# Filler matmuls of constants in the first third, an early activation table, and an order remade with the DMA lanes counted

## The chip, the cores and the metric

The kernel runs on one core of a Trainium2 chip. The metric is the device time of one execution in microseconds; the table of the profile gives the three runs of the kernel before and the one that was profiled.

## The reference

Two stages follow each other. The first is attention over 8 batches and 8 heads, with 1152 keys of 64 channels; the queries are averaged in pairs first, so that 576 are left. The second is a layer over the 4608 rows that come out of it: the maximum of three products, and a product of that.

```python
q_pool = q.reshape(B, H, S // factor, factor, D).mean(axis=3)
scores = scale * np.matmul(q_pool, k.transpose(0, 1, 3, 2))
scores = scores - np.max(scores, axis=-1, keepdims=True)
attn = np.exp(scores)
attn = attn / (np.sum(attn, axis=-1, keepdims=True) + 1e-09)
return np.matmul(attn, v).astype(np.float32)
...
h = np.maximum(np.maximum(x @ w1, x @ w2), x @ w3)
return (h @ w_out).astype(np.float32)
```

Here x is the attention's output with the eight heads of a query side by side (512 channels), w1 to w3 are 512 x 768 and w_out is 768 x 512. All values are float32.

## The kernel before, in words

**Units.** The attention is cut into 64 units, d = 0 to 63. A unit holds a pair of heads (two heads side by side), one batch, and half of the 576 queries, 288. For each of its nine blocks of 128 keys (kk = 0 to 8), TensorE (PE) makes the scores of both heads with four matmuls of 288 columns (`product` in `scores`, lines L578 and L579: the queries are split into a high and a low part, and so are the keys), into one of two PSUM buffers `pqk`. ScalarE (ACT) copies a block to SBUF (L588, into `s`, which holds three blocks) and VectorE (DVE) takes the running maximum `acc` (L594 for the first, L597). A PSUM buffer is free again when its copy and its maximum are done, so the product of block kk waits for the maximum of block kk-2.

After the ninth block the maximum over keys is turned (`rows`, L688, into `pmt`), reduced by DVE (L694), turned back and spread over the partitions (`bcast`, L704, into `pmb`), and DVE subtracts it from the scores (`sub`, L733, six instructions per unit: three for the first 345 columns, whose maximum lies in PSUM pool `ps_a`, and three for the other 231, in `ps_b`). From unit 16 on (`TURN`) the maximum goes another way, by `fold`, `turn` (L648), `summit` and a matmul L714. ACT makes the exponential (L739), and PE multiplies by the values (`pav`, L784). The sums over keys come from PE for d < 8 (L828) and later from GpSimd (POOL, L754 and L756).

**The second stage** is cut into chunks of tokens. A chunk needs x of all four head pairs, and the weights, which arrive as 64-bit numbers and are split into a high and a low part: ACT L975, L988 and L999, DVE L978 and L983, POOL L991 and L1002. Until the first chunk can start, shortly before 213 us, PE has attention alone to do; after that there is always some of the second stage's work (L1068, L1123) to put between.

**What sets the order.** Every piece of work is a `Step` with the engine it runs on, a cost and the steps it waits for. `arrange` (from L211) plays the steps through on a clock per engine and, at each turn, gives the engine that is free first the ready step of the lowest rank. Ranks come from the tables `RANK` and `NUDGE`. Steps are then written out in that order, so each engine's queue is fixed. The planner knows that TensorE's clock halves: it sums the columns streamed in windows of 4096 / 1200 = 3.41 us (`WINDOW`) and takes a step for twice as long when the window before held fewer than 3072 (`BUSY`).

```python
            while rest > 1e-9:
                w = int(at / WINDOW + 1e-9)
                while len(streamed) < w + 2:
                    streamed.append(0.0)
                slow = 2 if w == 0 or streamed[w - 1] < BUSY else 1
```

A DMA step gets a tail, the time until its data has landed. Most loads, and the moves of split keys (`kc`, L498) and queries (`qq`, L506), are issued by SyncE (SP); the four moves of the first half of the queries of unit 0 by ACT. There are eight completion semaphores for DMAs, used in turn, here called lanes: an issue waits until the DMA that had its lane before has landed. The planner before does not know of these.

At the start, ACT's first instruction is the cast L461 of the queries; the load of its activation table stands right before it and comes behind the same wait.

Of the kernel before, what the change touches and what calls it, by code (L numbers as in the profile page):

```python
# [18 lines left out]
P = 128  # L19
# [20 lines left out]
    "qk": -1610.0615,  # L40
    "cp": -180.1672,
    "mx": -1253.2067,
    "rows": -786.0194,
    "turn": -1110.3828,
    "top": 469.0602,
    "diag": -189.5205,
    "red": 77.8083,
    "bc": -879.861,
    "sub": 3840.475,
    "exp": 984.6769,  # L50
    "keys": -2399.561,
    "av": 683.8571,
    "xcopy": -1571.289,
    "psum": 782.1931,
    "eps": 214.1172,
    "inv": 1557.6025,
    "xm": -150.8782,
    "load": -1024.6367,
    "prep": 2386.9581,
    "move": 1089.3258,  # L60
    "split": -86.6507,
    "ffn": 707.8881,
    "rate": 5.1716,
    "mm": 974.547,
    "fetch": 157.873,
    "evac": -1776.9799,
    "hhigh": 675.1121,
    "hlow": -1456.4392,
    "conv": 1545.6563,
    "rate0": 0.2612,  # L70
    "first_qk": -105.5392,
    "first_cp": 492.9138,
    "first_mx": 996.4585,
    "first_sub": 621.8249,
    "first_exp": 463.1478,
    "first_keys": -3171.6001,
    "first_av": -465.3423,
    "first_xcopy": 820.1949,
    "first_psum": 3176.8613,
    "first_inv": 117.4318,  # L80
    "first_xm": -1228.9986,
    "first_load": -1485.6615,
    "first_prep": 53.3922,
    "first_move": -618.3481,
    "first_split": 1939.7866,
# [102 lines left out]
BUSY = 3072  # L188
EARLY = 16
THIRDS = 7  # L190
LENT = 8
SUMS = 8
SPLIT = 8
IDLE = 0
APART = 0
SWITCH = 0.2

class Step:  # L200
# [10 lines left out]
def arrange(plan, slots):  # L211
# [12 lines left out]
    free = {k: [0.0] * n for k, n in slots.items()}  # L224
    parked = {k: [] for k in slots}
    order = []
    streamed = [0.0]
    mode = 0
    wire = 0.0

# [977 lines left out]
```

## Time and profile before

| | |
|---|---|
| median of three runs | 1421.44 us (1420.52 to 1423.86) |
| profiled execution, its own time | 1425.01 us |
| span of its instructions | 1423.2 us |
| mean granted TensorE clock over the span | 0.986 |
| busy in the span: PE, DVE, ACT, POOL | 1365.0, 1001.9, 915.3, 1069.1 us |
| busy from 0 to 213 us: PE, DVE, ACT | 168.45, 153.06, 157.39 us |

PE is an abbreviation for TensorE's matmuls, PEld for its weight loads, which overlap them. A row of the windows view gives, for a stretch in microseconds from the span's start, its length, then the busy time of each engine with its number of instructions, then the clock that TensorE was granted (1.00 is full speed), the share of time in which the DMA engines worked, and what they moved. A stretch with no record of the clock is shown as 1.00; there the distance between neighbouring matmuls tells the rate. A row of the timeline gives start, duration, engine, line, operation and tiles, and in brackets how long the engine had been idle before it and what ended that. A row of the groups gives the count after x, then busy time and mean nanoseconds of one, then idle time before.

### The profile page before, as it was taken

To read this page: it belongs to the slowest core of one execution; us is meant where nothing else is said; L and a number is where in the kernel's file an instruction comes from. 1 tells how busy PE (TensorE), PEld (TensorE's weight loads), DVE (VectorE), ACT (ScalarE), POOL (GpSimd) and SP (SyncE) were. 2 spreads that over 40 slices of the span, in tenths; PEclk is the share of its full clock that TensorE was granted. 3 is DMA by queue.
4 is the path that set the end of the run, shared out by engine and by line. 5 is a ranking of instruction groups with operands and counts; after the bars stand their busy time and mean duration, and the time that the engine had idled before them with its cause. 6 is when DMAs were issued, how large, how long until landed. Compare 5 with 4: busy or idle time off the path is not lost.

```text
span 1423.2 us, 24396 instructions
## 1 busy us (share of the span) xinstructions
PE 1365.0 (96%) x8608; PEld 1063.3 (75%) x8608; DVE 1001.9 (70%) x1355; ACT 915.3 (64%) x1520; POOL 1069.1 (75%) x843
## 2 busy tenths in 40 slices
PE   4878889999999999999999999999999999999999
PEld 3555567777777777776777777777877777778999
DVE  4778777766777878887778877777877778862110
ACT  3878787656766777767666776666766666661211
POOL 1344468879888999899898998899789988783210
PEclk9999889999999999999999999999999999999999
DMA  6678787655566756664567556765666466515451
GB/s 185 190 255 236 222 261 203 178 180 155 139 197 191 197 145 182 205 188 127 164 191 195 157 166 190 193 195 143 189 189 181 130 180 190 160 38 177 146 169 50
DMA packets 117353, 250.13 MB, mean 176 GB/s; under 512 B 15728, under 2 KB 75504, under 8 KB 117232
## 3 DMA queue, kind: packets, MB, share of 16 engines
q1 hardware_dynamic: 116656, 247.99, 59.4%
q8 instruction: 69, 1.13, 0.3%
q10 hardware_dynamic: 576, 0.59, 0.2%
q14 instruction: 52, 0.43, 0.1%
HBM read 154.14 MB, written 18.87 MB: 122 GB/s over the span
## 4 chain that ended last, share of the span: by engine, by line
PE 85%; DVE 4%; ACT 3%; DMA 3%; issue 2%; POOL 2%; SPq 1%; ACTq 0%; POOLq 0%; DVEq 0%
PE ph L1068 30%; PE pav L784 19%; PE pqk L578 11%; PE po L1123 10%; PE pqk L579 9%; DVE acc L597 2%; PE psum L798 2%; ACT s L588 1%; DVE s L733 1%; PE pmb L714 1%; DMA w<-in_win_dram 1%; PE psum L828 1%; ACT s L739 1%; POOL ksum L756 1%; DMA qq<-qraw 1%
## 5 line engine op out<-in xcount | busy, mean ns | idle before, releaser
L756 POOL TENSOR_TENSOR ksum<-ksum,s 128x576 f32<-128x576 f32 x392 | 557.9, 1423 | 20.9 <-ACT s L739 2.5
L1068 PE MATMUL ph<-xh,w 128*128 128x512 f32 (+2 forms) x1440 | 460.5, 372 | 0.3 <-ACT hm L1087 0.3
L733 DVE TENSOR_TENSOR s<-s,pmb 128x864 f32<-128x864 f32 (+2 forms) x384 | 395.5, 1045 | 41.6 <-PE pmb L714 36.3
L588 ACT COPY s<-pqk 128x576 f32<-128x576 f32 x576 | 359.1, 639 | 100.8 <-PE pqk L579 96.5
L597 DVE TENSOR_TENSOR acc<-acc,pqk 128x576 f32<-128x576 f32 x448 | 334.7, 747 | 125.7 <-ACT s L588 121.5
L578 PE MATMUL pqk<-qq,kc 128*128 128x288 f32 x1152 | 346.0, 317 | 49.7 <-DVE acc L597 20.4
L739 ACT ACTIVATE s<-s 128x864 f32<-128x864 f32 (+2 forms) x384 | 353.7, 932 | 53.6 <-DVE s L733 51.4
L579 PE MATMUL pqk<-qq,kc 128*128 128x288 f32 x1152 | 327.6, 301 | 0.0
L578 PEld LDWEIGHTS pqk<-qq,kc 128*128 128x128 f32 x1152 | 222.8, 193 | 121.4 <-issue 37.1
L784 PE MATMUL pav<-s,v 128*64 128x288 f32 x2304 | 303.9, 417 | 0.6 <-DVE w L983 0.6
L1068 PEld LDWEIGHTS ph<-xh,w 128*128 128x128 f32 x1440 | 262.9, 188 | 37.1 <-issue 1.8
L1068 PE MATMUL ph<-xl,w 128*128 128x512 f32 (+2 forms) x720 | 266.9, 371 | 0.0
L784 PEld LDWEIGHTS pav<-s,v 128*64 128x64 f32 x2304 | 163.8, 140 | 117.8 <-issue 15.3
L579 PEld LDWEIGHTS pqk<-qq,kc 128*128 128x128 f32 x1152 | 224.4, 195 | 11.6
L1099 POOL TENSOR_TENSOR h<-hm,h 128x512 fp32r<-128x512 f32 (+2 forms) x60 | 70.9, 1181 | 98.7 <-ACT h L1096 98.5
L1068 PEld LDWEIGHTS ph<-xl,w 128*128 128x128 f32 x720 | 135.6, 188 | 10.4
L1089 DVE TENSOR_TENSOR hm<-hm,ph 128x512 f32<-128x512 f32 (+2 forms) x120 | 75.2, 626 | 95.5 <-PE ph L1068 92.1
L1123 PE MATMUL po<-h,wo_hi 128*128 128x512 f32 (+2 forms) x480 | 139.2, 374 | 0.2 <-ACT ob L1139 0.2
L754 POOL TENSOR_TENSOR ksum<-s 128x576 f32<-128x576 f32 x56 | 80.7, 1441 | 69.7 <-ACT s L739 69.6
L793 ACT COPY xr<-pav 128x288 f32<-128x288 f32 x64 | 25.5, 399 | 147.3 <-PE pav L784 147.1
L472 POOL TENSOR_TENSOR kraw<-kraw 128x1152 fp32r<-128x1152 f32 x31 | 82.7, 2667 | 46.8 <-ACT kraw L468 29.6
L805 DVE RECIPROCAL rs<-rs 128x288 f32<-128x288 f32 (+1 forms) x64 | 96.5, 1507 | 23.4 <-ACT rs L802 21.5
(69 smaller groups left out, 1169.6 us busy)
## 6 DMA issues: line engine op xcount, KB each, us to landing
w<-w_split SPq DMA_DIRECT2D x162, 512.0 KB, 3.8
kc<-kraw SPq DMA_DIRECT2D x384, 96.0 KB, 3.2
qq<-qraw SPq DMA_DIRECT2D x252, 144.0 KB, 3.7
v<-in_vr_dram SPq DMA_DIRECT2D x32, 576.0 KB, 3.8
kraw<-in_kT_dram SPq DMA_DIRECT2D x31, 576.0 KB, 5.7
qraw<-in_qT_dram SPq DMA_DIRECT2D x31, 576.0 KB, 4.0
w<-in_win_dram SPq DMA_DIRECT2D x18, 512.0 KB, 4.9
w_split<-wc SPq DMA_DIRECT2D x18, 512.0 KB, 5.0
```

The costliest lines, as they stand in the source:

```text
L472: vec[e].tensor_tensor(lo.bitcast(F32R), lo, o.hl[:, 0, x:y], op=ALU.subtract)
L578: nc.tensor.matmul(ps[:, h - hs[0], :QH], w, qq[:, 0, h], start=True, stop=False)
L579: nc.tensor.matmul(ps[:, h - hs[0], :QH], w, qq[:, 1, h], start=False, stop=True)
L588: nc.scalar.copy(o.s[kk // 3][:, kk % 3, slice(*hs)], o.ps[kk, hs][:, :, :QH])
L597: nc.vector.tensor_tensor(acc, acc, ps, op=ALU.max)
L733: nc.vector.tensor_tensor(s, s, o.pb[h][:, None, :w].broadcast_to([P, 3, w]), op=ALU.subtract)
L739: nc.scalar.activation(s, s, AF.Exp, scale=SCALE)
L756: vec[e].tensor_tensor(o.ksum, o.ksum, x, op=ALU.add)
L784: nc.tensor.matmul(o.pav[64 * h : 64 * h + 64, :QH], pr.v[:, kk, h], o.s[kk // 3][:, kk % 3, h], start=(kk == 0), stop=(kk == NK - 1),)
L805: nc.vector.reciprocal(o.rs, o.rs)
L1068: nc.tensor.matmul(t.ps[:, : hi - lo], w[:, a, kk], xx[:, kk, lo:hi], start=(kk == 0 and i == 0), stop=(kk == 3 and i == 2),)
L1123: nc.tensor.matmul(t.ps[:, : hi - lo], ww[:, kk, ms], hh[kk // 3][:, kk % 3, lo:hi], start=(kk == 0 and i == 0), stop=(kk == 5 and i == 2),)
```

## The change

Three things are done, and the order is made anew.

**Fillers.** Where the planner sees PE idle before the next step, within the first `FILL_END` = 500 us, and the window holds fewer than `BUSY` columns, it puts in matmuls of constants (`idle`, L1183 to L1186): 64 columns of the identity matrix against the identity, or against a matrix of ones with 64 columns where PE has just worked on half the array. Their output, `junk`, is never read. It lies in the last 128 columns of a PSUM bank that is now one tile for the whole kernel, `bank`; the first 384 columns, `bank_a`, take the place of the pool `ps_a`, for `pmt` and `pmb` of the first 345 columns. Because 128 columns are gone, `turn` and `summit` write to the front of the bank. There are 208 fillers: 163 with the identity as weights and 45 with the ones; 48 of them stand ahead of the first product.

**Table.** An exponential of one column of `eps` is ACT's first instruction, so that the table's load waits for no data.

**Lanes.** A DMA step starts, for the planner, no earlier than the eighth DMA before it has landed.

**Order.** `RANK` and `NUDGE` hold new numbers throughout (one line of each is shown).

```diff
-    "qk": -1610.0615,
+    "qk": -1495.1031,
...
-    "av.0": 687.59, "av.1": 431.26, "av.10": -61.53, "av.11": -1121.69, "av.12": 92.79, "av.13": 2220.5,
+    "av.0": -115.98, "av.1": -51.15, "av.10": -108.01, "av.11": -670.85, "av.12": 1006.11, "av.13": 2186.58,
...
-IDLE = 0
+FILL = 256
+FILL_END = 500
+LANES = 8
...
+    landed = [0.0] * LANES
...
-    while len(order) < len(plan):
+    todo = len(plan)
+    while todo:
...
+        if e == "pe" and FILL and clock[e] < min(FILL_END, t):
+            at = clock[e]
+            while True:
+                w = int(at / WINDOW + 1e-9)
+                while len(streamed) < w + 2:
+                    streamed.append(0.0)
+                if streamed[w] >= BUSY:
+                    at = (w + 1) * WINDOW + 1e-7
+                    if at >= t:
+                        break
+                    continue
+                took = (FILL / 2400 + 0.02) * (2 if w == 0 or streamed[w - 1] < BUSY else 1)
+                if at + took > t:
+                    break
+                streamed[w] += FILL
+                at += took
+                order.append((at, None, mode))
+        if s.size:
+            t = max(t, landed[-LANES])
...
+            landed.append(wire + 1.8)
...
+    bank = ps_a.tile([P, 512], F32, name="bank_a")
+    bank_a, junk = bank[:, :384], bank[:, 384:]
...
+    nc.scalar.activation(cpool.tile([P, 1], F32, name="first"), eps, AF.Exp)
...
-            o.pb[0] = ps_a.tile([P, 512], F32, tag="a", name=f"pmb{d}_0")
-            nc.tensor.transpose(o.pb[0][:, QH : QH + P], crest[d % 2], ident)
+            o.pb[0] = bank_a
+            nc.tensor.transpose(o.pb[0][:, :P], crest[d % 2], ident)
...
-                o.pt[h] = pools[h].tile([P, 512], F32, tag="ab"[h], name=f"pmt{d}_{h}")
+                o.pt[h] = ps_b.tile([P, 512], F32, tag="b", name=f"pmt{d}") if h else bank_a
...
-                o.pb[h] = pools[h].tile([P, 512], F32, tag="ab"[h], name=f"pmb{d}_{h}")
+                o.pb[h] = ps_b.tile([P, 512], F32, tag="b", name=f"pmb{d}_{h}") if h else bank_a
...
+    def idle(mode):
+        n = FILL // 4
+        rows, cols = (64, ones) if mode else (P, ident)
+        nc.tensor.matmul(junk[:rows, :n], cols, ident[:, :n], start=True, stop=True)
...
         for _, s, e in order:
-            s.fn(e)
+            if s is None:
+                idle(e)
+            else:
+                s.fn(e)
```

How it moves instructions is shown at three places. In these rows `pqk0_1` is unit 0, block 1; a row tells what is written and what is read, and in brackets the semaphores that the instruction waits for (the engine's name, or a DMA lane). Lines of the changed kernel are some twenty higher: L599 and L600 are the scores, L804 the values, L753 the subtraction, L609 ACT's copy.

The first place is PE's queue at its beginning, before the change:

```order
L578 MATMUL pqk0_0_174<-qq0_0_144,kc0_0_147 128x288 [waits DMAHW6_49,DMAHW7_49,DMAHW1_49,DMAHW0_49]
L579 MATMUL pqk0_0_174<-qq0_0_144,kc0_0_147 128x288
L578 MATMUL pqk0_0_174<-qq0_0_144,kc0_0_147 128x288 [waits DMAHW3_49,DMAHW5_49,DMAHW2_49,DMAHW0_49]
L579 MATMUL pqk0_0_174<-qq0_0_144,kc0_0_147 128x288
L578 MATMUL pqk0_1_181<-qq0_0_144,kc0_0_147 128x288
```

The same place of PE's queue after the change, up to the second block:

```order
L1186 MATMUL bank_a_94<-ident_95 128x64 [waits Pool_49]
L1186 MATMUL bank_a_94<-ident_95 128x64 x47
L599 MATMUL pqk0_0_220<-qq0_0_147,kc0_0_150 128x288 [waits DMAHW6_49,DMAHW7_49,DMAHW1_49,DMAHW0_49]
L600 MATMUL pqk0_0_220<-qq0_0_147,kc0_0_150 128x288
L599 MATMUL pqk0_0_220<-qq0_0_147,kc0_0_150 128x288 [waits DMAHW4_49,DMAHW5_49,DMAHW3_49,DMAHW2_49]
```

48 fillers, which wait for nothing but the identity matrix that POOL makes, have come in ahead of the first product.

The second place is ACT's queue at its beginning. `qraw0` and `kraw0` are the queries and keys of the first pair, which ACT casts (L461 and L468; L482 and L489 in the changed kernel) and whose halves the DMAs move into `qq0_0`. Before:

```order
L461 ACT_TABLE_LOAD [waits DMAHW0_49]
L461 CAST qraw0_130<-qraw0_130 128x288 [waits DVE_49]
L468 CAST kraw0_132<-kraw0_132 128x384 [waits DMAHW1_49]
L506 DMA qq0_0_144<-qraw0_130 64x2x288 [waits DVE_49]
L506 DMA qq0_0_144<-qraw0_130 64x2x288
L461 CAST qraw0_130<-qraw0_130 128x288 [waits DMAHW2_49,DVE_49]
L468 CAST kraw0_132<-kraw0_132 128x384 [waits DMAHW3_49]
L468 CAST kraw0_132<-kraw0_132 128x384 [waits DMAHW4_49]
L506 DMA qq0_0_144<-qraw0_130 64x2x288 [waits DMAHW5_49]
L506 DMA qq0_0_144<-qraw0_130 64x2x288 [waits DMAHW0_49]
```

ACT's queue at its beginning after the change:

```order
L387 ACT_TABLE_LOAD
L387 ACTIVATE first_104<-eps_102 128x1 [waits DVE_49]
L482 CAST qraw0_133<-qraw0_133 128x288 [waits DMAHW0_49,DVE_49]
L489 CAST kraw0_135<-kraw0_135 128x384 [waits DMAHW1_49]
L527 DMA qq0_0_147<-qraw0_133 64x2x288 [waits DVE_49]
L527 DMA qq0_0_147<-qraw0_133 64x2x288
L527 DMA qq0_0_147<-qraw0_133 64x2x288 [waits DMAHW4_49]
L527 DMA qq0_0_147<-qraw0_133 64x2x288 [waits DMAHW5_49]
L482 CAST qraw0_133<-qraw0_133 128x288 [waits DMAHW2_49,DVE_49]
L489 CAST kraw0_135<-kraw0_135 128x384 [waits DMAHW3_49]
```

The table's load has lost its wait, and the third and fourth move of the queries have come ahead of the casts of the other query half and of the second and third part of the keys.

The third place is PE's queue at the end of unit 2's scores, where unit 1's values are mixed in (`pav1`). Before:

```order
L784 MATMUL pav1_543<-s1_0_255,v0_194 64x288 x4
L578 MATMUL pqk2_7_559<-qq1_0_317,kc1_2_342 128x288 [waits DVE_49]
L579 MATMUL pqk2_7_559<-qq1_0_317,kc1_2_342 128x288
L578 MATMUL pqk2_7_559<-qq1_0_317,kc1_2_342 128x288
L579 MATMUL pqk2_7_559<-qq1_0_317,kc1_2_342 128x288
L578 MATMUL pqk2_8_567<-qq1_0_317,kc1_2_342 128x288 [waits DVE_49]
L579 MATMUL pqk2_8_567<-qq1_0_317,kc1_2_342 128x288
```

The same end of unit 2's scores on PE after the change:

```order
L599 MATMUL pqk2_7_615<-qq1_0_420,kc1_2_450 128x288 [waits DVE_49]
L600 MATMUL pqk2_7_615<-qq1_0_420,kc1_2_450 128x288
L599 MATMUL pqk2_7_615<-qq1_0_420,kc1_2_450 128x288
L600 MATMUL pqk2_7_615<-qq1_0_420,kc1_2_450 128x288
L1186 MATMUL bank_a_94<-ident_95 128x64 [waits DVE_49]
L1186 MATMUL bank_a_94<-ident_95 128x64 x6
L599 MATMUL pqk2_8_638<-qq1_0_420,kc1_2_450 128x288 [waits PE_49]
L600 MATMUL pqk2_8_638<-qq1_0_420,kc1_2_450 128x288
```

Seven fillers have come between the blocks, and the first of them waits for DVE. Since `junk` and `bank_a` are one tile, a filler counts as a writer of the tile that DVE's subtraction reads: here it waits for the subtraction of unit 1 from `s1_2`, which stands behind the maximum of block 6 in DVE's queue. 27 groups of fillers have such a wait for DVE, and 10 subtractions of DVE wait for a filler in turn.

More of the change, by code (lines that the diff above doesn't have):

```diff
@@ L39 @@
 RANK = {
-    "qk": -1610.0615,
[L41 to L85, printed above, removed]
+    "qk": -1495.1031,
+    "cp": 59.6252,
+    "mx": -795.4198,
+    "rows": -884.2635,
+    "turn": -1391.2299,
+    "top": 1202.9278,
+    "diag": -1242.8229,
+    "red": -51.5927,
+    "bc": -1041.7961,
+    "sub": 4016.7319,
+    "exp": 1156.5563,
+    "keys": -2564.3934,
+    "av": 1420.6901,
+    "xcopy": -731.9903,
+    "psum": 1442.2799,
+    "eps": 64.1427,
+    "inv": 2145.5552,
+    "xm": -578.7354,
+    "load": -1554.9367,
+    "prep": 2701.617,
+    "move": 1738.2672,
+    "split": -84.4622,
+    "ffn": 768.468,
+    "rate": 4.6882,
+    "mm": 1532.7636,
+    "fetch": -298.6013,
+    "evac": -1037.2018,
+    "hhigh": 612.2296,
+    "hlow": -1655.1451,
+    "conv": 1058.5478,
+    "rate0": 1.462,
+    "first_qk": 283.3284,
+    "first_cp": -22.0406,
+    "first_mx": 198.0721,
+    "first_sub": 933.0186,
+    "first_exp": 126.2895,
+    "first_keys": -3301.6863,
+    "first_av": -1158.6745,
+    "first_xcopy": 808.7904,
+    "first_psum": 2911.6716,
+    "first_inv": 79.6498,
+    "first_xm": -697.1703,
+    "first_load": -1812.6465,
+    "first_prep": -907.8762,
+    "first_move": -1756.2913,
+    "first_split": 1822.6689,
 }
 NUDGE = {
[90 rows of a table removed]
[90 rows of a table added]
 }
@@ L293, in arrange @@
             s.tail = wire - s.end + 1.8
+            landed.append(wire + 1.8)
         order.append((t, s, e))
+        todo -= 1
         if s.give:
@@ L418, in tile_attention_ffn @@
         pass
-    def stream(e):
-        ps = ps_ff.tile([P, 512], F32, tag="ff", name="idle")
-        nc.tensor.matmul(ps[:, :P], ident, ident, start=True, stop=True)
-    for i in range(IDLE):
-        Step(plan, lambda: 1e5, [pe(213)], stream, [], take="ff", give="ff", cols=512)
     pairs = {}
@@ L630, in scores @@
         o.rows, o.subs, o.exps, o.pt, o.pb, o.m = [], [[], []], {}, {}, {}, {}
-        pools = (ps_a, ps_b)
         late = d >= TURN
@@ L646, in turn @@
         def turn(e):
-            o.pb[0] = ps_a.tile([P, 512], F32, tag="a", name=f"pmb{d}_0")
-            nc.tensor.transpose(o.pb[0][:, QH : QH + P], crest[d % 2], ident)
+            o.pb[0] = bank_a
+            nc.tensor.transpose(o.pb[0][:, :P], crest[d % 2], ident)
         def summit(e):
-            o.top = o.pb[0][:NB, QH + P : QH + P + SQ]
+            o.top = o.pb[0][:NB, P : P + SQ]
             nc.vector.tensor_reduce(
-                o.top, o.pb[0][:NB, QH : QH + P].rearrange("p (g k) -> p k g", g=4), axis=AX.X, op=ALU.max
+                o.top, o.pb[0][:NB, :P].rearrange("p (g k) -> p k g", g=4), axis=AX.X, op=ALU.max
             )
```

178 rows, old and new, of the table NUDGE are left out of this document.

## The prediction

> **What bounds the kernel now.** I read the page first, then the same rows by stage.
>
> ```profile
> span 1423.2 us, 24396 instructions
> ...
> PEclk9999889999999999999999999999999999999999
> ```
>
> In forty slices of the span the clock granted to PE falls under 0.9 in the fifth and sixth only, up to 213 us. The windows view, asked for the stretch before and the one behind, gives length, PE, weight loads, DVE, ACT and POOL, then the clock:
>
> ```profile
> 0.00:213.00 213.00, 168.45 (x1210) 115.76 (x1212) 153.06 (x238) 157.39 (x250) 90.00 (x77) 0.91 0.75 225
> 213.00:1423.00 1210.00, 1196.59 (x7402) 947.56 (x7398) 848.85 (x1118) 757.95 (x1270) 979.07 (x767) 1.00 0.57 167
> ```
>
> After 213 us PE idles for 13.4 of 1210 us: that part is PE's own work, and little can be won. Before, PE idles for 44.6 us and neither DVE (72%) nor ACT (74%) is full. PE's longest waits in that stage, but for the first loads, are its products' for DVE's running maximum (us, times, longest):
>
> ```profile
> PE pqk L578 <- DVE acc L597: 16.9, 19, 2.2
> ```
>
> Cut at the steps of the clock, the stage looks like this:
>
> ```profile
> 57.62:61.04 3.42, 0.85 (x5) 0.56 (x4) 3.42 (x6) 3.22 (x4) 1.94 (x2) 1.00 0.91 253
> 61.04:64.45 3.41, 3.33 (x14) 2.11 (x16) 3.41 (x5) 3.41 (x7) 0.00 (x0) 0.50 0.88 338
> ...
> 98.58:102.00 3.42, 1.66 (x18) 1.34 (x19) 3.42 (x7) 3.11 (x5) 1.89 (x2) 1.00 0.13 49
> 102.00:108.82 6.82, 6.16 (x24) 3.70 (x23) 6.79 (x10) 6.80 (x11) 5.19 (x4) 0.50 0.53 148
> ...
> 139.54:146.37 6.83, 5.68 (x22) 3.29 (x24) 6.33 (x9) 5.73 (x9) 5.15 (x5) 0.50 0.69 205
> 146.37:156.61 10.24, 9.76 (x92) 6.45 (x92) 6.08 (x9) 7.80 (x14) 4.71 (x4) 1.00 0.67 201
> ...
> 160.02:163.44 3.42, 3.42 (x15) 1.84 (x12) 3.42 (x8) 2.27 (x4) 0.00 (x0) 0.50 0.89 263
> 163.44:173.68 10.24, 10.24 (x100) 6.81 (x100) 7.42 (x13) 7.82 (x14) 2.42 (x3) 1.00 0.85 229
> ...
> 177.09:183.91 6.82, 6.29 (x25) 3.58 (x26) 6.33 (x9) 6.20 (x10) 6.04 (x5) 0.50 0.80 211
> 183.91:197.57 13.66, 12.76 (x116) 8.62 (x116) 9.15 (x15) 9.88 (x18) 5.45 (x5) 1.00 0.83 259
> ...
> 200.98:207.81 6.83, 5.54 (x20) 4.57 (x20) 6.08 (x10) 5.72 (x11) 6.52 (x7) 0.50 1.02 311
> ```
>
> It is a cycle. DVE has a burst of subtractions and is full for 3.4 us; PE, waiting, is busy for 0.85 or 1.66 of 3.42 us; then the clock is halved for one or two windows, in which PE is full again and does half as much; then PE works off its backlog, 96 to 100% busy, and DVE starves (22.65 of 34.14 us in the three stretches that follow, 66%).
>
> **The change part by part.**
>
> *Half-rate stretches.* The stretches at 0.50 in the stage are the five above and this one:
>
> ```profile
> 37.14:40.56 3.42, 3.24 (x14) 2.00 (x16) 3.42 (x5) 2.86 (x5) 0.00 (x0) 0.50 0.68 164
> ```
>
> PE is busy in them for 3.24 + 3.33 + 6.16 + 5.68 + 3.42 + 6.29 + 5.54 = 33.66 us (seven with 61.04). What the rate costs is read between neighbouring matmuls of 288 columns, first at the start, then at full clock:
>
> ```profile
> 16.20 0.44 PE L578 MATMUL pqk<-qq,kc 128*128 128x288 f32 x1
> 16.44 0.44 PE L579 MATMUL pqk<-qq,kc 128*128 128x288 f32 x1
> ...
> 48.28 0.29 PE L579 MATMUL pqk<-qq,kc 128*128 128x288 f32 x1
> 48.41 0.29 PE L578 MATMUL pqk<-qq,kc 128*128 128x288 f32 x1
> ```
>
> They are 240 ns apart against 130, so 46% of 33.66 us, 15.4 us, is the most that full clock gives back. Nothing is won inside these stretches where DVE is full, but the backlog behind them shrinks, and there PE's time is the kernel's. Two discounts: the fillers are placed on the planner's windows, and the chip's own lie otherwise, so I let two of the eleven half-rate windows stay (9/11); and where DVE is full again at once the backlog was hidden (I take 80% as on the path). 15.4 x 9/11 x 0.8 = 10.1: **10 us gained**, between 0 and 15.4.
>
> The Trainium skill (TensorE: Matmul & The Clock Gate, "Why this matters for your kernels") speaks against this part: it asks only that PE have no idle gap of over some 3 us between bursts. By that rule fillers in shorter gaps save nothing, and this term would be 0. The trace does not bear it out: the longest gap of PE in 98.58 to 102.00 is 2.31 us, and the clock fell all the same.
>
> ```profile
> 100.28 0.37 PE L578 MATMUL pqk<-qq,kc 128*128 128x288 f32 x1 [2.31 <-issue]
> ```
>
> *The start.* No step of the clock is recorded ahead of 33.73 us, but the 240 ns above show half rate there. Two products then take 2.85 us, by ACT's copies:
>
> ```profile
> 20.25 0.64 ACT L588 COPY s<-pqk 128x576 f32<-128x576 f32 x1 [1.11 <-PE pqk L579]
> ...
> 23.10 0.64 ACT L588 COPY s<-pqk 128x576 f32<-128x576 f32 x1 [1.12 <-PE pqk L579]
> ```
>
> Four matmuls less by 0.11 us each, twice, is 0.9 us of 2.85; copy and maximum stay in the loop with their waits, so I take 0.6 for a pair, over some five pairs: **3 us gained**, between 0 and 4.5. The table stands in the way of the first cast only:
>
> ```profile
> 3.91 0.46 DVE L458 TENSOR_TENSOR qraw<-qraw 128x288 f32<-128x288 f32 x1 [0.50 <-DMA qraw<-in_qT_dram]
> 3.96 1.28 ACT L461 ACT_TABLE_LOAD   x1 [3.96 <-DMA qraw<-in_qT_dram]
> ...
> 5.26 0.43 ACT L461 CAST qraw<-qraw 128x288 fp32r<-128x288 f32 x1
> ```
>
> The cast could start when the sum is done, at 4.37, instead of 5.26: 0.9 us. ACT then issues four moves of the queries ahead of the casts of the later keys; that brings the second head's queries forward and the moves of key parts 1 and 2 back, on SP as well, where all that stands behind them moves too. I take **1 us gained** for both together, between -1 (a key part becomes the last to arrive) and +2.
>
> *What the fillers cost.* The 48 ahead of the first product run while it waits for its DMA; their cover is that wait, to 12.6 us. Of the 160 others, 115 load 128 weight columns. The nearest row has weights of 96 columns and one moving column, so that it is paced by its weight loads:
>
> ```profile
> L815 PE MATMUL psum<-ones,ksum 128*96 128x1 f32 x96 | 9.0, 220 | 0.0
> ```
>
> 9.0 us by 96 is 94 ns for one record, and a float32 matmul is two (six in each of units 8 to 15 make the 96): 188 ns for a filler, where the planner counts 127 (256 / 2400 + 0.02). All 160 together are 30 us, in 44.6 us of idle time plus what the full clock frees, so most fit. They overrun their gaps by 160 x 0.061 = 9.8 us if each gap is as planned; a quarter on the path: **2.5 us lost**, between 0 and 9.8.
>
> *The false waits.* A filler in a group that waits for DVE holds everything behind it in PE's queue. At 17 of the 27 groups the next real instruction waits for the same or a later DVE instruction, or for ACT behind it: no cost. At ten it needs an earlier one, and the group waits for one subtraction more. DVE's rows from 34 to 213 us:
>
> ```profile
> L597 DVE TENSOR_TENSOR acc<-acc,pqk 128x576 f32<-128x576 f32 x63 | 47.0, 746 | 10.2 <-ACT s L588 9.8
> L733 DVE TENSOR_TENSOR s<-s,pmb 128x1035 f32<-128x1035 f32 x28 | 34.2, 1223 | 3.9 <-PE pmb L704 3.9
> L733 DVE TENSOR_TENSOR s<-s,pmb 128x693 f32<-128x693 f32 x27 | 23.2, 859 | 0.0
> ```
>
> Those ten groups hold 37 fillers, so a product comes later by 1.22 + 3.7 x 0.19 = 1.92 us. Its maximum waits for it on DVE, but DVE has the maximum before it (0.75) and often the shorter subtraction (0.86) to do: 1.61 us of cover. Left are 0.31 us by ten: **3 us lost**, between 0 and 19.2 (no cover). The ten subtractions that wait for a filler stand behind a maximum of the product just before that filler, and the product's copy and maximum, 0.64 + 0.75, are longer than most groups: nothing; at most 2 us.
>
> *The order.* No real matmul is added or dropped. After 213 us at most 13.4 us could be won; the lanes, now counted, should help SP's queue, but DMA is hardly named among PE's waits. I take 0, from -4 to +4. The bank's new layout costs nothing: `ps_a` had one buffer, so `turn` waited for the subtractions before as well.
>
> The sum against the profiled 1425.0 us (its span and 1.8 us around it): 10 + 3 + 1 - 2.5 - 3 = 8.5, so 1416.5 us. That execution lies 3.6 us above the median of the runs, 1421.4, so the forecast for the runs is **1412.9 us**.
>
> **The rivals.** *All of it comes through*: no half-rate window stays, and the overruns and false waits lie in DVE's bursts. 15.4 + 3 + 1 - 1 = 18.4 us, so 1403 us. For it: DVE and ACT have a quarter of the stage free. Against it: the planner cannot see the false waits.
>
> *The false wait takes the idle gap's place* (slower). DVE releases PE later, PE releases DVE later, at the ten places, all in subtractions of units 1 to 9. If the cover fails, 19.2 us are lost, and half of the fillers' overrun, 5 us, is on the path as well: with 14 gained that is 10 us more, so 1431 us. It decides from 11.5 us of lateness on the path (14 gained less 2.5 of overrun), 60% of the whole. For it: the waits for DVE are what PE's idle time is made of now. Against it: DVE's own queue of 1.61 us at each place.
>
> *The clock doesn't follow the fillers.* If a filler's 64 columns don't count, or fall into other windows than needed, the half-rate stretches stay, at the start too: 1 gained, 2.5 + 3 lost, so 1426 us; with the start at full clock, 1423. The skill's rule of the 3 us gap, above, comes to the same. Against it: the clock falls after windows with little streamed, and the fillers add up to eight matmuls just there.
>
> **How the numbers follow.** Forecast 0.52, all of it 0.25, false wait 0.13, clock 0.10. A measurement of this kernel tells 0.2%, 2.8 us, from no change: faster is under 1418.6, slower over 1424.3. The forecast's own range is 1407 to 1420 (its terms' halves); 0.46 of its 0.52 lies under 1418.6, and with the first rival faster is 0.71. Same is the 0.06 left of it, 0.04 of the clock's case and 0.03 of the false wait's with half its cover, together 0.13; slower is the rest, 0.16. The range from 1401 to 1425 leaves out the lower tail of the first rival, some 0.06, and 0.13 of the two on the other side.
>
> **What would show it.** Right: few windows at 0.50 before 200 us, matmuls 130 ns apart at the first scores, the second stage's first matmuls some 8 us earlier, the stretch behind them as long as before. Wrong: products behind the waiting groups with idle time released by DVE's subtraction, and DVE's idle time before its maximum above the 10.2 us shown; or 0.50 as often as before; or PE idle for more than 13.4 us in the later part.

## The result, and the profile after the change

The changed kernel takes 1441.36 us (median of four runs, 1439.98 to 1443.85), the kernel before beside it 1422.65 us (four runs). The ratio is 1.0126, 95% interval 1.0089 to 1.0163: slower, where the forecast was 1412.9 us and faster.

The profiled execution took 1443.85 us, with a span of 1442.1 us. This is its page: busy time and share of the span, then the span in forty slices.

```profile
span 1442.1 us, 25189 instructions
...
PE 1407.7 (98%) x9024; PEld 1114.7 (77%) x9024; DVE 1001.3 (69%) x1355; ACT 915.4 (63%) x1521; POOL 1067.4 (74%) x843
...
PEclk9989998999999999999999999999999999999999
```

PE is busy for 98% of the span, more than before, and the kernel is slower: part of that busy time is fillers. Two groups by line, over the whole span, give them apart (busy time, mean ns; then idle time before and what ended it):

```profile
L1186 PE MATMUL bank_a<-ident 128*128 128x64 f32 x326 | 56.6, 338 | 12.3 <-DVE s L753 10.0 <-POOL ident masks.py:199 1.4 <-DVE m L714 0.9
L1186 PE MATMUL bank_a<-ident,ones 128*64 128x64 f32 x90 | 8.7, 245 | 3.8 <-DVE s L753 3.8
```

A float32 filler leaves two records, so these are the 208 fillers, with records of 65.3 us. The records of neighbouring matmuls overlap, though, so the fillers are better priced by what they add. Counted from the records of the trace, the real matmuls by themselves keep PE busy for 1354.0 us, 11.0 us less than before (1365.0), and the fillers add 53.7 us to that. PE's idle time fell as well, from 58.2 to 34.4 us. So -11.0 - 23.8 + 53.7 = +18.9 us, which is the difference of the spans. The real matmuls took less because less of them ran at half rate (19.2 us in the first stage against 47.5, with all that lies ahead of the first record of the clock taken as half rate), and the fillers took nearly five times what that gave.

The same sum can be made for the first stage alone, up to the first matmul of the second stage: it started at 205.3 us before and starts at 232.5 us now. In the windows view a row gives the length, PE, weight loads, DVE, ACT and POOL, then the clock. This is the stage before:

```profile
0.00:205.30 205.30, 160.88 (x1170) 109.81 (x1171) 148.53 (x232) 151.02 (x240) 82.46 (x71) 0.91 0.75 224
```

And this is the stage after the change:

```profile
0.00:232.50 232.50, 214.42 (x1675) 169.13 (x1676) 162.34 (x251) 160.68 (x257) 94.62 (x78) 0.94 0.70 207
```

The same stretch of the changed kernel, for the fillers' line alone (length, PE, weight loads):

```profile
0.00:232.50 232.50, 62.54 (x394) 59.21 (x394) 0.94 0.70 207
```

The clock is higher, 0.94 against 0.91, and the stage is 27.2 us longer. A little of that is the new order, which puts more of the attention into it: 1675 - 394 = 1281 real records instead of 1170. With the new order and no filler (experiment 1) the same 1281 take 206.9 us, so 25.6 us come with the fillers. Two places show how. The first is the start. Before the change PE's first product stood here:

```profile
12.61 0.58 PE L578 MATMUL pqk<-qq,kc 128*128 128x288 f32 x1 [12.61 <-DMA qq<-qraw]
```

The timeline of PE after it:

```profile
1.35 20.74 PE L1186 MATMUL bank_a<-ident 128*128 128x64 f32 x96 [1.35 <-POOL ident masks.py:199]
21.85 0.59 PE L599 MATMUL pqk<-qq,kc 128*128 128x288 f32 x1
22.24 0.44 PE L600 MATMUL pqk<-qq,kc 128*128 128x288 f32 x1
22.48 0.44 PE L599 MATMUL pqk<-qq,kc 128*128 128x288 f32 x1
```

The 48 start fillers take 20.5 us from the first start to the first product, 214 ns for a record and 428 ns for a filler. The first product begins at 21.85 us instead of 12.6, and the scores are still 240 ns apart: PE was full for 20.74 us, and the clock had not risen.

The second place is a waiting group of 14 records (7 fillers) in unit 2. Rows of the timeline of PE, DVE and ACT, with other work between them left out:

```profile
67.24 1.23 DVE L753 TENSOR_TENSOR s<-s,bank_a 128x1035 f32<-128x1035 f32 x1
...
68.52 3.12 PE L1186 MATMUL bank_a<-ident 128*128 128x64 f32 x14 [2.14 <-DVE s L753]
...
71.40 0.59 PE L599 MATMUL pqk<-qq,kc 128*128 128x288 f32 x1
...
72.74 0.64 ACT L609 COPY s<-pqk 128x576 f32<-128x576 f32 x1 [3.34 <-PE pqk L600]
...
73.42 0.76 DVE L618 TENSOR_TENSOR acc<-acc,pqk 128x576 f32<-128x576 f32 x1 [3.68 <-ACT s L609]
```

PE idles for 2.14 us until DVE's subtraction has read the bank. Only then do the fillers start, and the product follows 2.88 us after their start. ACT's copy and DVE's maximum follow the product, and DVE has been idle for 3.68 us. The fillers did not fill the gap: they waited through it and ran behind it. The clock by stretches around this group:

```profile
64.45:68.71 4.26, 2.12 (x16) 1.42 (x12) 3.49 (x5) 3.49 (x6) 1.33 (x2) 1.00 0.00 0
68.71:75.53 6.82, 6.82 (x30) 4.90 (x29) 3.14 (x5) 2.86 (x5) 1.84 (x2) 0.50 0.47 151
```

PE was busy for 2.12 of 4.26 us in the stretch with the wait, and at its end the clock was halved, just when the fillers began. Over the stage, from 36 to 213 us, DVE's maximum tells the same as this one place; its idle time was 10.2 us before:

```profile
L618 DVE TENSOR_TENSOR acc<-acc,pqk 128x576 f32<-128x576 f32 x63 | 47.2, 749 | 16.9 <-ACT s L609 16.2
```

### The profile page after: what moved, and what is told of

It reads as the page before. It is cut to its first block, busy times and chain, and to the rows that moved or that the text cites. A ratio compares the mean times of both kernels' runs of the same rounds, so it can differ in the third digit from the quotient of the medians.

```text
span 1442.1 us, 25189 instructions
## 1 busy us (share of the span) xinstructions
PE 1407.7 (98%) x9024; PEld 1114.7 (77%) x9024; DVE 1001.3 (69%) x1355; ACT 915.4 (63%) x1521; POOL 1067.4 (74%) x843
## 4 chain that ended last, share of the span: by engine, by line
PE 83%; DVE 6%; ACT 3%; issue 2%; DMA 2%; POOL 2%; SPq 1%; ACTq 0%; DVEq 0%; POOLq 0%
PE ph L1088 28%; PE pav L804 18%; PE po L1143 10%; PE pqk L599 10%; PE pqk L600 9%; PE bank_a L1186 3%; DVE acc L618 3%; DVE s L753 2%; PE psum L818 2%; ACT s L609 2%; POOL ksum L776 1%; DMA kraw<-in_kT_dram 1%; PE psum L874 1%; ACT s L759 1%; PE bank_a L734 1%
## 5 line engine op out<-in xcount | busy, mean ns | idle before, releaser
L609 ACT COPY s<-pqk 128x576 f32<-128x576 f32 x576 | 358.8, 638 | 124.8 <-PE pqk L600 120.2
L599 PE MATMUL pqk<-qq,kc 128*128 128x288 f32 x1152 | 342.5, 314 | 13.1 <-DVE acc L618 7.7
L600 PE MATMUL pqk<-qq,kc 128*128 128x288 f32 x1152 | 323.4, 298 | 0.0
L804 PE MATMUL pav<-s,v 128*64 128x288 f32 x2304 | 297.0, 410 | 0.0
L599 PEld LDWEIGHTS pqk<-qq,kc 128*128 128x128 f32 x1152 | 220.1, 191 | 78.4 <-issue 29.9
L804 PEld LDWEIGHTS pav<-s,v 128*64 128x64 f32 x2304 | 162.1, 137 | 112.2 <-issue 8.8
L753 DVE TENSOR_TENSOR s<-s,bank_a 128x864 f32<-128x864 f32 (+1 forms) x192 | 209.1, 1092 | 38.1 <-PE bank_a L734 34.1
L600 PEld LDWEIGHTS pqk<-qq,kc 128*128 128x128 f32 x1152 | 220.6, 191 | 11.0
L753 DVE TENSOR_TENSOR s<-s,pmb 128x864 f32<-128x864 f32 (+1 forms) x192 | 192.1, 1001 | 0.2 <-PE pmb L724 0.2
```

The costliest lines, as they stand in the source:

```text
L599: nc.tensor.matmul(ps[:, h - hs[0], :QH], w, qq[:, 0, h], start=True, stop=False)
L600: nc.tensor.matmul(ps[:, h - hs[0], :QH], w, qq[:, 1, h], start=False, stop=True)
L609: nc.scalar.copy(o.s[kk // 3][:, kk % 3, slice(*hs)], o.ps[kk, hs][:, :, :QH])
L753: nc.vector.tensor_tensor(s, s, o.pb[h][:, None, :w].broadcast_to([P, 3, w]), op=ALU.subtract)
L804: nc.tensor.matmul(o.pav[64 * h : 64 * h + 64, :QH], pr.v[:, kk, h], o.s[kk // 3][:, kk % 3, h], start=(kk == 0), stop=(kk == NK - 1),)
```

## The experiments

The theory after this result: the loss is made of the waiting groups and of the start, and the new order, the table and the fillers' own time are small beside them. Rivals: the new order itself is slower; or the fillers are slow simply because PE has no room for them; or the fillers, waits or not, never lift the clock.

The experiments were timed against the kernel before, in three sets with a kernel before of 1424.61, 1424.07 and 1424.71 us; beside the changed kernel it took 1422.65. A trace shows one execution of each kernel. The column "difference" is the median less the median of the kernel before in its own set.

| kernel | median us | difference | ratio, 95% interval |
|---|---|---|---|
| as changed | 1441.36 | +18.7 | 1.0126 (1.0089 to 1.0163) |
| 1 no fillers | 1417.62 | -7.0 | 0.9954 (0.9939 to 0.9969) |
| 2 no start fillers | 1435.66 | +11.1 | 1.0074 (1.0047 to 1.0102) |
| 3 the waits only | 1432.78 | +8.2 | 1.0054 (1.0033 to 1.0075) |
| 4 before, with the early table | 1423.87 | -0.7 | 0.9992 (0.9982 to 1.0002) |
| 5 wide start only | 1417.56 | -6.5 | 0.9953 (0.9934 to 0.9972) |
| 6 two banks, later fillers | 1415.68 | -8.4 | 0.9940 (0.9918 to 0.9961) |
| 7 two banks, light fillers, wide start | 1414.03 | -10.0 | 0.9932 (0.9917 to 0.9947) |
| 8 fillers without waits only | 1417.99 | -6.1 | 0.9944 (0.9925 to 0.9963) |
| 9 the start fillers only | 1426.62 | +1.9 | 1.0012 (0.9999 to 1.0025) |
| 10 half of the start fillers only | 1418.34 | -6.4 | 0.9952 (0.9938 to 0.9967) |
| 11 two banks, light fillers, no start | 1413.31 | -11.4 | 0.9918 (0.9903 to 0.9934) |
| 12 as 7, with 42 wide matmuls | 1415.66 | -9.0 | 0.9933 (0.9917 to 0.9948) |

**1. No fillers.** The order, the table and the lanes of the change stay; `idle` is never called.

```diff
             if s is None:
-                idle(e)
+                pass
```

> The changed kernel with none of its 208 fillers; order, early table and the one bank stay. Theory of the fillers (the start at half rate and the waits for DVE are the loss, the new order is as good as the old): 1418 to 1423 us, half-rate windows as many as before, first product at 12 us. Rival, the new order itself is slower: 1433 us or more, as the second stage still begins late.

Measured: 1417.62 us, 0.46% faster than before. The new order is not the cause; with the table and the one bank it is worth 7 us. The row of its first stage:

```profile
0.00:206.90 206.90, 171.95 (x1281) 120.92 (x1282) 159.55 (x250) 159.51 (x257) 93.70 (x78) 0.95 0.77 229
```

Its clock is 0.95 without a single filler: the recorded windows at 0.50 in this stage come to 23.9 us, against 37.5 us before.

**2. No start fillers.** The 160 later ones stay as they are.

```diff
+        begun = False
         for _, s, e in order:
+            begun = begun or (s is not None and e == "pe")
             if s is None:
-                idle(e)
+                if begun:
+                    idle(e)
```

> The changed kernel without the 48 fillers ahead of the first product. Theory that the start is a loss of its own: the first product comes 9 us earlier, and the kernel takes 1432 us (9 less than the changed one). Rival, the later fillers and their waits or the order set the end, and the start is hidden behind them: within 3 us of 1441.

Measured: 1435.66 us. The later fillers cost 18 us over the kernel without any; the start takes the rest, 18.7 - 11.1 = 7.6 us. That is rough, since the intervals of the two overlap; experiment 9 prices the start by itself.

**3. The waits only.** One filler of one column where a group waits for DVE, and no other, so that the wait is there and the filler nearly not. The trace has 56 records of them, 28 fillers, one more than the 27 groups.

```diff
-        n = FILL // 4
+        n = 1
...
             if s is None:
-                idle(e)
+                if begun and read[0]:
+                    idle(e)
+                    read[0] = False
```

(`read[0]` is set by the steps of DVE that read `bank_a`, and cleared by PE's real writes of it.)

> No fillers but one in each of the 27 groups that wait for DVE, with one column in place of 64: the waits without the fillers' time. Theory of the waits: some 6 to 10 us slower than without any filler, so 1427 to 1432 us. Rival, PE's time on the fillers is the loss: as without fillers, 1418 to 1423 us.

Measured: 1432.78 us, 15.2 us over the kernel without fillers. PE's longest wait up to 230 us in the first experiment, but for the first loads (us in total, times, longest):

```profile
PE pqk L599 <- DVE acc L618: 15.9, 21, 1.7
```

The same view with the waits only:

```profile
PE bank_a L1191 <- DVE s L758: 14.5, 13, 2.1
...
PE pqk L600 <- DVE acc L619: 5.9, 12, 1.2
```

Most of the idle time has changed hands, from the maximum that a product needs to a subtraction that it doesn't need, and 10 us for the maximum became 14.5 for the subtraction. The same place as above shows what it does to the product. The timeline without fillers:

```profile
57.73 1.22 DVE L753 TENSOR_TENSOR s<-s,bank_a 128x1035 f32<-128x1035 f32 x1
57.86 0.40 PE L599 MATMUL pqk<-qq,kc 128*128 128x288 f32 x1 [1.51 <-DVE acc L618]
```

The timeline with the waits only:

```profile
59.56 1.23 DVE L758 TENSOR_TENSOR s<-s,bank_a 128x1035 f32<-128x1035 f32 x1
...
60.84 0.38 PE L1191 MATMUL bank_a<-ident 128*128 128x1 f32 x2 [2.15 <-DVE s L758]
...
61.09 0.38 PE L600 MATMUL pqk<-qq,kc 128*128 128x288 f32 x1
...
62.87 0.75 DVE L619 TENSOR_TENSOR acc<-acc,pqk 128x576 f32<-128x576 f32 x1 [0.82 <-ACT s L610]
```

Counted from the start of the subtraction the product begins after 0.13 us without fillers, after 1.53 us with the wait, and after 4.16 us in the changed kernel (71.40 less 67.24). Of the 1.53 us the little filler itself is 0.25 at most (60.84 to 61.09). The product used to run beside the subtraction; now it comes behind it.

The windows at 0.50 in its first stage come to 47.8 us, twice as many as without fillers, and the mean clock over the span is 0.979 to 0.982 in its four executions, against 0.986 to 0.994 in the ten without fillers: fillers that wait make idle time of the very kind behind which the clock is halved here.

**4. The kernel before with the early table.**

```diff
     nc.vector.memset(eps, EPS)
+    nc.scalar.activation(cpool.tile([P, 1], F32, name="first"), eps, AF.Exp)
```

> The kernel before with the early activation alone. Theory: the first cast comes 0.9 us earlier and all behind it, 1421.5 us. Rival, the first product waits for a DMA that does not move: 1422.6 us, no change.

Measured: 0.7 us faster, with an interval that takes in no change. So of the 7 us of the first experiment some 6 are the new order's. The first cast came earlier, at 4.60 instead of 5.26 us, but ACT's first copy of scores did not. Before:

```profile
16.44 0.64 ACT L588 COPY s<-pqk 128x576 f32<-128x576 f32 x1 [7.50 <-PE pqk L579]
```

With the early table:

```profile
16.43 0.64 ACT L589 COPY s<-pqk 128x576 f32<-128x576 f32 x1 [7.68 <-PE pqk L580]
```

**5. A wide start.** No filler of the planner, and ahead of everything 28 matmuls of 128 columns.

```diff
+        for i in range(28):
+            nc.tensor.matmul(junk, ident, ident, start=True, stop=True)
```

> The changed kernel without its 208 fillers, but with 28 matmuls of 128 columns ahead of the first product. Theory that the 48 fillers left the clock low because their weight loads took twice their streaming: streaming without gaps lifts the clock within two windows, the 28 end by 10 us, the first scores are 130 ns apart, and the kernel takes 1415 us (2 to 3 less than with no fillers). Rival, constants do not count for the clock: 428 ns for each, the first product at 13.4 us, the scores 240 ns apart, 1417.6 us.

Measured: 1417.56 us, as without them. Stretches of its start, cut at the steps of the clock, the first of which is at 5.70 us (what lies ahead of it has no record and is shown as 1.00):

```profile
1.36:5.70 4.34, 4.34 (x20) 4.34 (x21) 2.97 (x12) 1.70 (x4) 0.00 (x0) 1.00 0.75 185
5.70:12.52 6.82, 4.23 (x38) 4.04 (x36) 0.74 (x2) 0.00 (x0) 0.00 (x0) 1.00 0.95 242
12.52:33.00 20.48, 16.29 (x59) 14.02 (x60) 9.28 (x15) 9.97 (x16) 3.53 (x2) 0.50 0.60 174
```

Twenty records in 4.34 us, then about twice as many in 4.23: the wide fillers do lift the clock. But the timeline of PE shows that nothing follows them:

```profile
1.36 8.57 PE L1194 MATMUL bank_a<-ident 128*128 128x128 f32 x56 [1.36 <-POOL ident masks.py:199]
14.75 0.58 PE L600 MATMUL pqk<-qq,kc 128*128 128x288 f32 x1 [4.82 <-DMA qq<-qraw]
```

They end at 9.9 us, the first product waits for its queries until 14.75 us, and from 12.52 us the clock is at one half again.

**6. Two banks.** The second small pool becomes one tile as well, `bank_b`, and each later filler writes to the spare columns of whichever bank DVE read longer ago. No start fillers; number, size and planned place of the 160 are those of the change.

```diff
-    bank_a, junk = bank[:, :384], bank[:, 384:]
+    bank2 = ps_b.tile([P, 512], F32, name="bank_b")
+    bank_a, bank_b = bank[:, :384], bank2[:, :384]
+    spare, read, seen = [bank[:, 384:], bank2[:, 384:]], [0, 0], [0]
...
+        junk = spare[read[1] < read[0]]
```

> The 160 later fillers alone, each written to the one of two PSUM banks that DVE read longer ago; the second bank is made one tile as the first. Theory of the waits: most of their 15 us goes, half-rate windows stay as few as with fillers, 1415 to 1422 us. Rival, PE's time on the fillers: still over 1430 us.

Measured: 1415.68 us. The same fillers without most of their waits cost 19.5 us less than in the second experiment (-8.4 against +11.1). The same place in its timeline:

```profile
60.53 1.77 PE L1196 MATMUL bank_b<-ident 128*128 128x64 f32 x14
...
61.65 1.23 DVE L761 TENSOR_TENSOR s<-s,bank_a 128x1035 f32<-128x1035 f32 x1
...
62.11 0.38 PE L605 MATMUL pqk<-qq,kc 128*128 128x288 f32 x1
```

Now the fourteen records begin in the gap, 1.12 us ahead of the subtraction, and the product begins 0.46 us after its start. From the first record to the product is 1.58 us, 0.113 for a record and 0.226 for a filler at full clock. Its first stage in the windows view:

```profile
0.00:208.88 208.88, 186.16 (x1578) 143.51 (x1579) 161.13 (x251) 160.17 (x258) 93.84 (x78) 1.00 0.76 227
```

And the fillers in that stage:

```profile
0.00:208.88 208.88, 37.52 (x298) 35.06 (x298) 1.00 0.76 227
```

From 27.5 us to the end of the span no window is at one half in this trace: here the fillers do all that they were put in for. The 37.5 us of their records overlap with real matmuls, as at the place above, where they end at 62.30 us and the product begins at 62.11. Counted from the records as before, PE's real matmuls by themselves take 160.0 us of the stage, 11.9 less than without fillers, and its idle time is 22.7 us, 12.2 less. But the fillers add 26.1 us, so the stage ends 2 us later than without them (208.9 against 206.9), and the whole gain, 1.4 us by the differences, is not separated from zero (the intervals of 1 and 6 overlap). No run has the two banks without fillers, so what the second bank does by itself is not known.

**7. Light fillers.** As 6, with the matrix of ones as weights for every filler (64 weight columns), and the wide start of 5.

```diff
-        rows, cols = (64, ones) if mode else (P, ident)
-        nc.tensor.matmul(junk[:rows, :n], cols, ident[:, :n], start=True, stop=True)
+        nc.tensor.matmul(junk[:64, :n], ones, ident[:, :n], start=True, stop=True)
```

> As the kernel with two banks, with all later fillers on 64 weight columns (half the weight load) and the 28 wide matmuls at the start. If fillers help at all once they neither wait nor overrun, this is the fastest: 1411 to 1415 us. Rival, idle PE time and half-rate windows of the first 213 us lie off the path: as without fillers, 1417.6 us or a little above.

Measured: 1414.03 us, faster than both kernels.

**8. Only the fillers that wait for nothing.** Of the change's own groups those are left that no reading of DVE stands before. The trace has 42 records of them, 21 fillers, and all but one of these start in the first 33 us.

```diff
-                idle(e)
+                if begun and not read[0]:
+                    idle(e)
```

> Only the 24 fillers that wait for nothing, nearly all in the scores of unit 0. Theory: they lift the clock there or at least do no harm, 1415 to 1418 us. Rival, PE's time on fillers costs: 1420 us.

Measured: 1417.99 us, no different from no fillers at all.

**9 and 10. The start by itself.** No planned fillers; 48 of the change's start fillers, then 24.

```diff
+        for i in range(48):
+            idle(False)
```

> The new order and the early table with no later filler, and the 48 start fillers of the change (64 columns) put ahead of everything on TensorE. It prices the start by itself. Theory (the start fillers don't lift the clock and run into the products, which begin 9 us late): about 5.7 us over the kernel with no fillers, so 1423, with the clock at one half until at least 22 us and the first product at 21.9. Rival (the start is only dear because what follows it in the changed kernel waits as well): 1417 to 1419.

> As the run before it with 24 start fillers instead of 48, which at 428 ns each end at about 11.6 us, before the first product can begin. Theory (the overrun is the price, and narrow fillers do not count toward the clock): 1417.6, as with no fillers, first product at 13 to 15 us, and no step of the clock to full before 20 us. Rival (narrow fillers do lift the clock, and 48 were only too many): 1414 to 1416, with a step to full before 12 us.

Measured: 1426.62 us with 48, 8.9 us over no fillers, more than in company (7.6) and more than expected. The first product begins 8.7 us later than with no fillers (21.86 against 13.18 us). With 24 it is 1418.34 us, no different from none. The start on PE with 48, by the timeline:

```profile
1.36 20.74 PE L1186 MATMUL bank_a<-ident 128*128 128x64 f32 x96 [1.36 <-POOL ident masks.py:199]
21.86 0.59 PE L599 MATMUL pqk<-qq,kc 128*128 128x288 f32 x1
```

And with 24:

```profile
1.36 10.50 PE L1186 MATMUL bank_a<-ident 128*128 128x64 f32 x48 [1.36 <-POOL ident masks.py:199]
13.41 0.58 PE L599 MATMUL pqk<-qq,kc 128*128 128x288 f32 x1 [1.55 <-DMA qq<-qraw]
```

With 24 the queries' move ends the wait, as before, and the first record of full clock is at 30.45 us, as late as with none (31.22); with 48 it is at 39.52. So both parts of the theory hold: the overrun is the price, and fillers of 64 columns with 128 weight columns do not lift the clock here.

**11 and 12. The start of the best version.** As 7 without its wide start, and with 42 wide matmuls instead of 28.

> Two banks for the attention's small products, each later filler with 64 weight columns into the bank that VectorE read longer ago, and no start filler. It tells what of the gain of the best version so far (1414.0) is its wide start and what its lighter fillers. If the wide start gives its whole lead over the version with two banks and the change's own fillers: 1415.7. If the lighter fillers give it: 1414.0.

> As the best version so far, with 42 instead of 28 matmuls of 128 columns at the start, which at 0.107 us a record at full clock end at about 12.5 us, where the first product can begin. In the version with 28 the clock rose at 4.9 us and fell at 11.72, for 6.83 us, after the fillers had ended at 9.55. Theory (the clock follows the array's streamed columns): no fall there, the first scores run at full rate, some 3 us of half rate gone, up to 1.5 us less than with 28: 1412.5 to 1414. Rival (the scores there wait for their loads anyway, so that rate is hidden): 1414, no change.

Measured: 1413.31 us without, the fastest of all, and 1415.66 us with 42. So the wide start gives nothing of the lead, and the lighter fillers are what is left for it; the step from 6 to 11 alone is not separated from zero (their intervals overlap). The first stage of 11 in the windows view:

```profile
0.00:203.69 203.69, 180.19 (x1579) 130.94 (x1580) 160.85 (x251) 159.44 (x257) 93.45 (x77) 1.00 0.78 232
```

And its fillers alone:

```profile
0.00:203.69 203.69, 26.86 (x298) 21.26 (x298) 1.00 0.78 232
```

Their records take 26.9 us where those of 6 take 37.5. PE's real matmuls by themselves take 159.4 us, 12.5 less than without fillers, the fillers add 20.8, and the stage ends 5.2 us earlier than in 6. Against no fillers this gain is measured (0.9918 against 0.9954, with intervals that do not meet). With 42 the clock did what the theory said, and the time did not. Its timeline of PE at the first scores:

```profile
13.10 0.37 PE L606 MATMUL pqk<-qq,kc 128*128 128x288 f32 x1 [0.62 <-DMA qq<-qraw]
13.30 0.29 PE L607 MATMUL pqk<-qq,kc 128*128 128x288 f32 x1
14.43 0.37 PE L606 MATMUL pqk<-qq,kc 128*128 128x288 f32 x1 [0.84 <-DMA qq<-qraw]
14.64 0.29 PE L607 MATMUL pqk<-qq,kc 128*128 128x288 f32 x1
14.77 0.29 PE L606 MATMUL pqk<-qq,kc 128*128 128x288 f32 x1
```

The first scores are 130 ns apart, at full rate, and still wait for the queries' moves. A fast start is worth nothing that these runs can show; whether the 42 cost something (the intervals of 11 and 12 overlap) is left open.

The table gives PE's time up to the second stage's first matmul, in us, counted from the records of each trace: the real matmuls by themselves, what the fillers add to that, and the rest, in which PE idles. The real matmuls are the same in all rows, but for one record.

| kernel | first stage | real matmuls | added by fillers | idle |
|---|---|---|---|---|
| 1 no fillers | 206.9 | 172.0 | 0 | 35.0 |
| as changed | 232.5 | 162.8 | 51.6 | 18.1 |
| 2 no start fillers | 226.6 | 165.3 | 30.8 | 30.5 |
| 3 the waits only | 221.1 | 177.6 | 5.9 | 37.6 |
| 6 two banks | 208.9 | 160.0 | 26.1 | 22.7 |
| 11 two banks, light fillers | 203.7 | 159.4 | 20.8 | 23.5 |

## Why the prediction was wrong, by its own steps

By differences to the kernel before, the change comes apart as follows: order and table -7.0 (1), the waits +15.2 (3 less 1), the rest of the later fillers +2.9 (2 less 3, whose intervals overlap), the start +7.6 (changed kernel less 2; 8.9 by itself in 9); together +18.7. The forecast had 8.5 us gained.

*The false waits* are the step that failed, and the largest: 3 us lost in the sum, 15.2 measured, within its bound of 19.2. What failed is the cover. DVE's own queue was to hide 1.61 of 1.92 us at each of ten places. At the place shown the lateness was 1.4 us with the wait alone and 4.0 us in the changed kernel, since the seven fillers ran at half rate; DVE had idled for 0.82 and 3.68 us when its maximum came. The sum took the fillers behind the wait at a full-clock price, though behind such waits the clock was halved (47.8 us of windows at one half in 3), and it took the loop of product, copy and maximum as DVE's alone, though after a late product DVE cannot go on before the copy. And it had no term for the clock that the waits cost: by the table PE idled only 2.6 us longer with the waits alone than without fillers, and the real matmuls took 5.7 us more. Two things were not measured apart: whether the other 17 groups cost nothing, as the prediction had it, and what the little fillers of the third experiment cost by themselves, which at 0.25 us each is at most 7.0 of the 15.2 us.

The sign given for it came out: idle time released by DVE's subtraction, and 16.9 instead of 10.2 us of idle time before DVE's maximum. The rival *the false wait takes the idle gap's place*, at 0.13 and 1431 us, names the mechanism that happened. It is 10 us short; the start, which it had as 3 us gained and which lost 7.6, makes 10.6 of that.

*The start* failed as well, and in sign: 3 us gained in the sum, 7.6 lost. The cover named for the 48 fillers was the wait for the first DMA, to 12.6 us. The sum never set their length against that cover. At the 0.188 us of a filler from its own row they would take 9.0 us and fit; at the half rate which it had itself read off the first scores they take 48 x 0.428 = 20.5 us. And the 3 us weren't there: at full rate, with 42 wide matmuls, nothing was gained. The rival *the clock doesn't follow the fillers* was right for the start alone.

*Half-rate stretches* and *what the fillers cost* were sized apart, 10 gained and 2.5 lost. The first was about right: with most of the waits gone (6 against 1) no half-rate window is left behind the start, and the real matmuls by themselves took 11.9 us less, where 10.1 was taken and 15.4 the most. (The prediction speaks of five half-rate stretches and one more; its rows, and its sum, have seven.) What came of it was 1.4 us, because the second term failed. A filler took 0.226 us at full clock and 0.428 at half, not 0.188, but the larger error is the room: most of the fillers' time was to lie in idle gaps, with a quarter of 9.8 us of overrun on the path, and of the 26.1 us that they added 12.2 came out of idle time and 13.9 did not. With the light fillers it was 11.5 of 20.8 us, and 4.4 us were gained. The trace agrees with the prediction against the rule of the 3 us gap (the Trainium skill, TensorE: Matmul & The Clock Gate, "Why this matters for your kernels"): in the stretch from 64.45 to 68.71 us above, PE's longest gap was 2.14 us, PE was busy for half of the time, and the clock fell. The prediction's own gap of 2.31 us begins at 97.97 us, 0.61 us ahead of the stretch that it names; it is under 3 us all the same.

*The order* was 0 with 4 us either way, and gained about 6, a little outside. It was taken for neutral since PE does the same work, and PE's busy time is the same (1365.7 us in 1, 1365.0 before). What fell is PE's idle time, from 58.2 to 52.2 us. The first stage ends 1.6 us later, but it has 1281 records in place of 1170, and PE idles in it for 35.0 us in place of 44.4; behind it PE idles 3.5 us more than before. The fewer half-rate windows, 23.9 against 37.5 us, cannot be taken for the reason: the old order with the early table (4) has 27.3 us of them in its trace, and its 0.7 us are no clear gain. Which steps of the order do it was not tried, so the cause of this gain stays open.

*The table*, with ACT's order, was put at 1 us gained. The table alone gave 0.7 us, not separated from nothing, and the copies show none of it: the first stands at 16.43 us in 4 and at 16.44 before. ACT's order was not run alone. In 1 its four moves hold ACT's queue from 5.45 to 12.68 us, so that the next cast starts at 12.77 us instead of 7.68; the first copy comes at 15.68 us all the same, 0.8 us earlier than before.

## What to carry to other kernels

A filler shares its memory with something. Before putting work into an idle gap, ask what the work itself waits for: if it is released by what ends the gap, or by something later, it fills nothing and comes on top. Price it at the clock of the place where it runs, which behind a gap can be the slow one, and set the whole of its time, not only its overrun, against what the faster clock gives back: here 12 us of PE's time was bought with 26 us of fillers, and with lighter ones 12.5 us with 21 (6 and 11, against the first stage without fillers); only what fell into idle time, some 12 us, was free.

## What the runs showed of the hardware

Busy PE is not enough to raise the clock. Fillers of 64 columns with 128 weight columns kept PE busy for 20.74 us on end, at 214 ns a record, and the first record of full clock stands at 24.33 us, behind the first scores; in 9, without the later fillers, it stands at 39.52. Matmuls of 128 columns with the same weights raised it at 5.70 us, 4.3 us after the first, and the stretch shown above has 20 records in 4.34 us of half rate, some 217 ns each: the same time for twice the columns, so at 64 columns the weight load sets the pace. The light fillers, with half the weight columns, bear that out: from one record to the next are 107 ns at half rate and 58 at full (medians in run 11), against 213 and 112 with 128 weight columns (run 6). The Trainium skill (TensorE: Matmul & The Clock Gate, "What you observe") puts the rise at around 4 us of sustained matmuls; the wide ones come near it, with 4.3, 3.5 and 3.1 us in 5, 7 and 12, and the narrow ones, with 20 us, do not. That it is the columns streamed in a time that count is an inference. What speaks for it besides the two widths is that with the light fillers among the first scores (11) the clock is full from 17.99 us, with those of 128 weight columns (6) from 27.51 and with none from 31.22; but that is one trace of each. The later fillers of 64 columns, between scores, did hold a clock that was up.

A matmul into columns that nobody reads waits for a reader of other columns of the same bank: the waits for `s L753` above are all of that kind. It is the program that waits, on a semaphore. The Trainium skill (PSUM — Partial Sum Buffer, "PSUM bank collisions raise a hardware error") gives the reason: two engines must not be in the same 32 partitions of one bank at once, disjoint columns or not. No run here shows what a collision would do.
